# Attention feeding a squared-ReLU network: first-batch loads and projections in smaller parts, and one normalize moved a step earlier

## The chip, the cores and the metric

The kernel runs on one core of one Trainium2 chip. The metric is the device time of one execution in microseconds (us), so lower is better. Times are medians of several executions. A profiled execution also has a span, from its first to its last instruction; here the span is about 1.8 us shorter than the time of the same execution (482.0 against 483.81 in the profile of the kernel before).

Engines are named as the profile names them: PE is TensorE's matmul, PEld its weight load, DVE is VectorE, ACT is ScalarE, POOL is GpSimd (it issues most loads here), SP is SyncE.

## The reference

Linear attention with 64 projected keys feeds a two-layer network (cut to what matters):

```python
k_proj = np.einsum('ks,bhsd->bhkd', E, k)          # 8 batches, 8 heads, 1024 rows, head size 64
v_proj = np.einsum('ks,bhsd->bhkd', F, v)
scores = scale * np.matmul(q, k_proj.transpose(0, 1, 3, 2))
# ... softmax over the 64 projected keys
attn_out = np.matmul(attn, v_proj)
x = attn_out.transpose(0, 2, 1, 3).reshape(8192, 512)
h = np.maximum(x @ w_in, 0.0)                      # w_in is 512 x 2048
return h * h @ w_out                               # w_out is 2048 x 512
```

## The kernel before

Every batch is worked in "steps" of TensorE work of the two-layer network. The attention of the next batch is slipped in between those steps by tables that name a step and what to do there. Batches 2 to 6 carry the attention of the batch after them by the table `PIECES`. The first batch has nothing to hide behind: its attention stands ahead of the network, and so it is done in halves, and the first four blocks of the hidden layer are "opened" column group by column group as soon as parts of x exist.

The loads of the first batch, in the order in which they are issued:

```python
    def load_heads(t, src, g):
        s = slice(4 * g, 4 * g + 4)
        nc.gpsimd.dma_start(t[:, s], rows(src, 0)[:, s])
    # ...
    for g in range(2):
        load_heads(K_first, k, g)
    # ...
    load_q_half(0, slice(0, H))
    for g in range(2):
        load_heads(V_first, v, g)
    # ...
    for j in (0, 2, 1, 3):
        if j in (1, 3):
            load_q_half(1, slice(0, 4) if j == 1 else slice(4, 8))
        for g in range(2):
            nc.gpsimd.dma_start(w_in_sb[j][:, g], w_in_view[:, g, :, j * fw:(j + 1) * fw])
```

The stages of the first batch. `filler` is spare TensorE work, there only to keep the engine busy:

```python
        def first_stages(self):
            # ... filler
            self.project_k(0)
            # ... transpose_k(0), project_k(1), transpose_k(1), filler between
            for g in range(2):
                self.half_transpose_q(0, g, ffn_psum)
            for g in range(2):
                self.half_scores(0, g)
                self.half_exponentials(g)
            self.project_v(0)
            self.copy_v(0)
            self.half_sums(0, apart=True)
            self.half_sums(1)
            self.half_reciprocals(0)
            self.half_reciprocals(1)
            self.half_values(0)
            self.half_normalize(0, 0, 0)
            self.project_v(1)
            self.copy_v(1)
            self.half_normalize(0, 0, 1)

        def last_of_first(self):          # called one step into the network
            self.half_values(1)
            self.half_normalize(0, 1, 0)
            self.half_normalize(0, 1, 1)
```

The opening of the first four hidden blocks; `cb` is one of four column groups of x, and each normalize makes one of them:

```python
                def rest():
                    opening((3,), (0,))
                    for cb in range(1, NCB):
                        opening(range(4), (cb,), cb == NCB - 1)
                steps[0:4] = [lambda: opening(range(3), (0,)), rest, lambda: None, lambda: None]
```

The table for batches 2 to 6, and the two pools in PSUM (the memory that matmuls write to, in banks) whose buffers decide who waits:

```python
    aps = ctx.enter_context(tc.tile_pool(name="aps", bufs=2, space=bass.MemoryType.PSUM))   # attention
    fps = ctx.enter_context(tc.tile_pool(name="fps", bufs=4, space=bass.MemoryType.PSUM))   # network
    # ...
    PIECES = {
        # ...
        23: "sums 0, values 0 0, reciprocals 0", 26: "normalize 0 0",
        28: "scores 2, scores 3, exponentials 2", 29: "exponentials 3",
        # ...
    }
```

The softmax here doesn't subtract the row's maximum and nothing guards it: scores larger than these inputs give would overflow.

Of the kernel before, what the change touches and what calls it, by code (L numbers as in the profile page):

```python
# [8 lines left out]
P = 128  # L9
F32 = mybir.dt.float32  # L10
BF16 = mybir.dt.bfloat16
AF = mybir.ActivationFunctionType
# [8 lines left out]
def kernel(  # L21
# [11 lines left out]
    nc = tc.nc  # L33

    B, H, S, D = q.shape
    KP = E.shape[0]
    C = H * D
# [5 lines left out]
    NCB = C // P  # L43
# [29 lines left out]
    def ffn_psum(name, shape=(P, 512), dtype=F32):  # L73
        return fps.tile(list(shape), dtype, tag="ffn", name=name)

    def rows(src, b):
        return src[b].rearrange("h (p i) d -> p h (i d)", i=NI)
# [7 lines left out]
    for src in (E, F):  # L85
        t = relu_pool.tile([KP, S], F32, tag="h_relu", name="e_f32")
        nc.sync.dma_start(t[:], src[:])
        e_f32.append(t)
    K_first, V_first, Q_first = (
        qkv_pool.tile([P, H, NI * D], BF16, name=n) for n in ("K_sb", "V_sb", "Q_sb"))  # L90

    def load_heads(t, src, g):
        s = slice(4 * g, 4 * g + 4)
        nc.gpsimd.dma_start(t[:, s], rows(src, 0)[:, s])

    def load_q_half(c, h):
        s = slice(c * TH, (c + 1) * TH)
        nc.gpsimd.dma_start(Q_first[:, h, s], rows(q, 0)[:, h, s])

    for g in range(2):  # L100
        load_heads(K_first, k, g)
    ident = const_pool.tile([P, P], BF16, name="ident")
    make_identity(nc, ident[:])
    load_q_half(0, slice(0, H))
    for g in range(2):
        load_heads(V_first, v, g)
    nc.scalar.preload_act_table_set("natural_log_exp_and_others")
    ones = const_pool.tile([P, 32], BF16, name="ones")
    nc.vector.memset(ones[:], 1.0)
# [3 lines left out]
    w_in_view = moe_w_in.rearrange("(g p e) f -> p g e f", p=P, e=2)  # L113
    w_out_view = moe_w_out.rearrange("(fb p) m -> p fb m", p=P)
    WP = 4
    fw = FF // WP
    w_in_sb = [wpool.tile([P, 2, 2, fw], BF16, name=f"w_in_{j}") for j in range(WP)]
    wo = [wpool.tile([P, HFB, DM], BF16, name=f"w_out_{j}") for j in range(2)]
    for j in (0, 2, 1, 3):
        if j in (1, 3):  # L120
            load_q_half(1, slice(0, 4) if j == 1 else slice(4, 8))
        for g in range(2):
            nc.gpsimd.dma_start(w_in_sb[j][:, g], w_in_view[:, g, :, j * fw:(j + 1) * fw])
    for n in range(4):
        nc.gpsimd.dma_start(
            wo[n // 2][:, 4 * (n % 2):4 * (n % 2) + 4, :], w_out_view[:, 4 * n:4 * n + 4, :])
# [1 line left out]
    def w_in_blk(cb, fb):  # L128
        n = fw // P
        return w_in_sb[fb // n][:, cb // 2, cb % 2, (fb % n) * P:(fb % n + 1) * P]  # L130

    ET, FT = (const_pool.tile([P, NI, KP], BF16, name=n) for n in ("ET", "FT"))

    def E_and_F():
# [17 lines left out]
        o, a, b = {"T1": (T1, W12, W11), "T2": (T2, W22, T1), "T3": (T3, W22, W12), "T4": (T4, W21, T2)}[name]  # L152
        nc.vector.tensor_tensor(out=o[:, js], in0=a[:, js], in1=b[:, js], op=ALU.subtract)

    LO, HI = slice(0, 64), slice(64, 128)

    PLACE = {(0, 0): (LO, 0), (0, 1): (HI, 0), (1, 0): (HI, 1), (1, 1): (LO, 1)}

    class Attention:
# [111 lines left out]
                )  # L271
            nc.vector.tensor_copy(self.kT[:, s], ps[:])

        def project_v(self, g):
            if g == 0:
                self.vp = proj_pool.tile([P, H, 2, D // 2], BF16, name="vp")
            s = slice(4 * g, 4 * g + 4)
            ps = self.ps["vp", g] = ffn_psum("ps_v", (P, C // 2))
            vv = self.V[:, s].rearrange("p h (i d) -> p h i d", i=NI)
            for i in range(NI):  # L280
                for o in (LO, HI):
                    nc.tensor.matmul(
                        ps[o, :], lhsT=FT[:, i, :], rhs=vv[:, :, i, :], start=i == 0, stop=i == NI - 1)

        def copy_v(self, g):
            s = slice(4 * g, 4 * g + 4)
            nc.vector.tensor_copy(
                self.vp[:, s].rearrange("k h e d -> k e h d"),
                self.ps["vp", g][:].rearrange("k (h d e) -> k e h d", h=H // 2, e=2))

        def half_transpose_q(self, c, g, psum):
            ps = psum("ps_q", (P, 4, 2, P), BF16)
# [63 lines left out]
        def first_stages(self):  # L356
            def filler(n):
                ps = ffn_psum("ps_fill")
                for _ in range(n):
                    nc.tensor.matmul(ps[:], lhsT=ET[:, 0:2, :], rhs=ET[:], start=True, stop=True)  # L360

            filler(2)
            self.project_k(0)
            filler(1)
            self.transpose_k(0)
            self.project_k(1)
            filler(2)
            self.transpose_k(1)
            filler(1)
            for g in range(2):  # L370
                self.half_transpose_q(0, g, ffn_psum)
            for g in range(2):
                self.half_scores(0, g)
                self.half_exponentials(g)
            self.project_v(0)
            self.copy_v(0)
            self.half_sums(0, apart=True)
            self.half_sums(1)
            self.half_reciprocals(0)
            self.half_reciprocals(1)  # L380
            self.half_values(0)
            self.half_normalize(0, 0, 0)
            self.project_v(1)
            self.copy_v(1)
            self.half_normalize(0, 0, 1)

        def last_of_first(self):
            self.half_values(1)
            self.half_normalize(0, 1, 0)
            self.half_normalize(0, 1, 1)  # L390

        def second_half(self, stage, g):
            if stage == 0:
# [15 lines left out]
    PIECES = {  # L409
        1: "copy_kp", 2: "copy_vp", 4: "copy_v_down",  # L410
        20: "scores 0, scores 1, exponentials 0", 21: "exponentials 1",
        23: "sums 0, values 0 0, reciprocals 0", 26: "normalize 0 0",
        28: "scores 2, scores 3, exponentials 2", 29: "exponentials 3",
        47: "values 0 1, sums 1, reciprocals 1", 48: "normalize 0 1",
        53: "values 1 0, values 1 1", 54: "normalize 1 0", 55: "normalize 1 1",
# [16 lines left out]
        53: "values 1 0, values 1 1", 54: "normalize 1 0", 55: "normalize 1 1",  # L432
    }
    SECOND_HALF = {
        1: "last_of_first", 7: "second_half 0 0", 9: "second_half 1 0", 10: "second_half 0 1",
        11: "second_half 2 0", 12: "second_half 1 1", 13: "second_half 3 0",
        15: "second_half 2 1", 16: "second_half 3 1",
    }
# [17 lines left out]
    def ffn_groups(b, xT):  # L456
        def first(ch, fb, ps, cbs):
            for cb in cbs:
                nc.tensor.matmul(  # L459
                    ps[:], lhsT=w_in_blk(cb, fb), rhs=xT[:, cb, :, 2 * ch:2 * ch + 2],  # L460
                    start=(cb == 0), stop=(cb == NCB - 1),
                )
# [24 lines left out]
        def chunk(ch):  # L487
# [9 lines left out]
            def begin():  # L497
                st["hsq"] = hsq_pool.tile([P, 2, HFB, TCH], BF16, name="hsq")
                if b:
                    begin_sums()  # L500
# [4 lines left out]
            def square(k, n, ps):  # L505
                hsq = st["hsq"]
                if n == 0:
                    st["r"] = relu_pool.tile([P, 2, TCH], F32, name="h_relu")
                r = st["r"]
                nc.scalar.activation(r[:, n], ps[:], AF.Relu)  # L510
                if n == 0:
                    return
                (h, j), (h1, _) = pairs[k]
                o = hsq[:, :, j, :] if h != h1 else hsq[:, h, j:j + 2, :]
                if k in ON_SCALAR.get((b, ch), ()):
                    nc.scalar.activation(o, r[:], AF.Square)
                    return operands_after(k)
                multiply = lambda: nc.vector.tensor_tensor(out=o, in0=r[:], in1=r[:], op=ALU.mult)  # L518
                if b == 0 and ch == 0 and k in (4, HFB - 1):
                    held.append(multiply)  # L520
                    return
                multiply()
                operands_after(k)

            def operands_after(k):
                if b and 4 <= k < 7:
                    operands(0, (k - 4,))
                if b and k == 7:
                    operands(0, (3,))
                    operands(1, (0,))  # L530
# [14 lines left out]
            def opening(fbs, cbs, last=False):  # L545

                if "open" not in st:
                    begin()
                    st["open"] = {}
                for n in fbs:  # L550
                    if n not in st["open"]:
                        st["open"][n] = ffn_psum("ps_h")
                    h, j = pairs[n // 2][n % 2]
                    first(ch, HFB * h + j, st["open"][n], cbs)
                    if last:
                        square(n // 2, n % 2, st["open"][n])

            steps = [lambda k=k, n=n: step1(k, n) for k in range(HFB) for n in range(2)]
            if b == 0 and ch == 0:
                def rest():  # L560
                    opening((3,), (0,))
                    for cb in range(1, NCB):
                        opening(range(4), (cb,), cb == NCB - 1)
                steps[0:4] = [lambda: opening(range(3), (0,)), rest, lambda: None, lambda: None]
            elif b + ch == 1:
                def two():
                    if held:
                        held.pop()()
                    opening((0, 1), (2,))
                    opening((0, 1), (3,), True)  # L570
                steps[0:4] = [lambda: opening(range(4), (0, 1)), two] + [
                    lambda n=n: opening((n,), (2, 3), True) for n in (2, 3)]
# [108 lines left out]
        steps = f0 + f1 + s0 + s1  # L681
# [69 lines left out]
```

## Time and profile before

| | before |
|---|---|
| time, median of 3 runs | 484.76 us (484.01 to 484.77) |
| span of the profiled execution | 482.0 us |
| TensorE busy with matmuls | 470.4 us, 98% |
| first opening matmul / last of the 16 | 20.01 / 23.70 us |
| a batch, from one to the next (batches 2 to 6) | 57.38 us |

From the page of the kernel before, the engines' busy time and the chain of waits by engine:

```profile
PE 470.4 (98%) x3614; PEld 293.1 (61%) x3614; DVE 313.2 (65%) x380; ACT 261.8 (54%) x414; POOL 33.2 (7%) x46
...
PE 93%; DVE 3%; ACT 2%; DMA 1%; issue 0%; SPq 0%
```

TensorE is the limit. But "98% busy" does not say how much is left to win: the Trainium skill, "Perfetto Trace Analysis", section "Identifying the Most-Contended Engine", says that matmul busy time is not a good measure of how close a kernel is to its limit, because matmuls are pipelined. This trace agrees: a 512-column matmul shows 0.38 us of duration, but the next one starts 0.216 us later. So only the distances between starts are read here. The 0.216 is also what "TensorE: Matmul & The Clock Gate", section "Wait — 56ns, not 53.3ns?", gives for 512 columns at the full clock (215.7 ns).

Now the timeline of the kernel before in the opening. The columns are start, length, engine, line, operation, output and inputs, count, and in brackets the engine's idle time before it and what ended it:

```profile
18.58 1.06 PE L282 MATMUL ps_v<-V_sb,FT 128*64 128x256 bf16 x16
...
19.27 0.69 DVE L350 TENSOR_TENSOR xT<-ps_att,rs 128x512 bf16<-128x512 f32 x1 [1.17 <-ACT rs L341]
...
19.88 0.41 DVE L287 CAST vp<-ps_v 128x256 bf16<-128x256 f32 x1
...
20.01 0.81 PE L459 MATMUL ps_h<-xT,w_in 128*128 128x512 bf16 x3 [0.37 <-DVE xT L350]
...
20.75 0.41 PE L319 MATMUL ps_att<-expT,vp 64*32 64x256 bf16 x16
...
21.10 4.26 PE L459 MATMUL ps_h<-xT,w_in 128*128 128x512 bf16 x18
...
22.01 1.79 PEld L459 LDWEIGHTS <-w_in 128*128 128x128 bf16 x9 [0.15 <-DMA w_in<-in_moe_w_in_dram]
```

TensorE projects the second half of V at 18.58, waits for the first normalize (19.27), starts three opening matmuls at 20.01, does the second group of values at 20.75 once V's copy (19.88) is done, and resumes the opening at 21.10. Some 0.5 us of idle time lie ahead of 20.01.

And the timeline of the kernel before at the second group of scores in batch 2, which is the same in batches 3 to 6:

```profile
164.41 0.69 DVE L595 TENSOR_TENSOR o_sb<-ps_z,p_b 128x512 f32<-128x512 f32 x1 [4.22 <-ACT p_b L591]
165.02 1.22 DVE L244 TENSOR_TENSOR xT<-ps_att,rs 128x1024 bf16<-128x1024 f32 x1
165.99 0.70 PE L204 MATMUL ps_att<-qT,kT 64*64 64x512 bf16 x8
...
166.29 0.11 PEld L204 LDWEIGHTS <-kT 64*64 64x64 bf16 x4 [0.18 <-DVE xT L244]
```

The normalize (line 244) stands behind an add (line 595) that can't start before 164.41. So it ends at 166.24. Its PSUM bank is what the second of the two score groups waits for: the groups start at 165.99 and 166.29, which is 0.30 apart, where the pair at 157.68 us, which waits for nothing, has 0.24.

### The profile page before, as it was taken

The page shows a single profiled execution, that of the slowest core. Times are in us where ns is not written, and L with a number is a line of the kernel's source. Part 1 is how long each engine was busy: PE and PEld are TensorE (multiplying, and loading weights), DVE is VectorE, ACT ScalarE, POOL GpSimd, SP SyncE. Part 2 cuts the span into 40 slices and gives each one's busy share as a digit, 9 for nine tenths or more (in the row PEclk, how much of TensorE's full clock was granted, in tenths as well). Part 3 has the DMA queues.
Part 4 walks back from the last instruction along what each step waited for, and adds up shares of the span by engine and source line. Part 5 has one row for each costly group of instructions (what it writes and reads, how often), then busy time and mean ns, then how long its engine had stood idle before and what let it go on. Part 6 is the DMA issues. An engine that isn't in the chain of part 4 may idle for free.

```text
span 482.0 us, 8383 instructions
## 1 busy us (share of the span) xinstructions
PE 470.4 (98%) x3614; PEld 293.1 (61%) x3614; DVE 313.2 (65%) x380; ACT 261.8 (54%) x414; POOL 33.2 (7%) x46
## 2 busy tenths in 40 slices
PE   4899999999999999999999999999999999999997
PEld 2544776475575746657475665747557474666656
DVE  1478855555958558493876748666594855948383
ACT  2488544758426664466635657176662756545351
POOL 6340020020020001000010000100000000000000
PEclk9999999999999999999999999999999999999999
DMA  9999989479989075931859147590712002020202
GB/s 162 204 204 207 170 184 203 124 128 227 172 124 238 6 176 89 192 80 64 145 87 229 13 121 131 90 196 1 173 3 81 20 1 88 1 88 0 88 0 88
DMA packets 72501, 55.46 MB, mean 115 GB/s; under 512 B 33936, under 2 KB 64656, under 8 KB 72464
## 3 DMA queue, kind: packets, MB, share of 16 engines
q0 software_dynamic: 30336, 29.36, 39.0%
q1 hardware_dynamic: 42128, 25.56, 21.2%
q8 instruction: 28, 0.46, 0.4%
q14 instruction: 9, 0.07, 0.0%
HBM read 59.24 MB, written 16.78 MB: 158 GB/s over the span
## 4 chain that ended last, share of the span: by engine, by line
PE 93%; DVE 3%; ACT 2%; DMA 1%; issue 0%; SPq 0%
PE ps_h L459 44%; PE ps_y L479 23%; PE ps_z L479 11%; PE ps_x L479 6%; PE ps_kv L178 3%; PE ps_att L219 2%; PE ps_att L204 2%; DVE hsq L518 1%; DMA e_f<-in_F_dram 1%; PE ps_k L260 1%; DVE s L473 1%; DVE xT L244 0%; ACT expT L313 0%; DVE xT L350 0%; ACT h_relu L510 0%; PE ps_fill L360 0%
## 5 line engine op out<-in xcount | busy, mean ns | idle before, releaser
L459 PE MATMUL ps_h<-xT,w_in 128*128 128x512 bf16 x1024 | 225.0, 379 | 0.4 <-DVE xT L350 0.4
L518 DVE TENSOR_TENSOR hsq<-h_relu 128x1024 bf16<-128x1024 f32 x123 | 150.0, 1223 | 76.7 <-ACT h_relu L510 76.1
L510 ACT ACTIVATE h_relu<-ps_h 128x512 f32<-128x512 f32 x256 | 149.8, 597 | 62.6 <-PE ps_h L459 62.4
L459 PEld LDWEIGHTS <-w_in 128*128 128x128 bf16 x1024 | 99.6, 98 | 117.9 <-issue 1.7
L479 PEld LDWEIGHTS <-s 128*128 128x128 bf16 x1024 | 98.5, 98 | 19.8 <-issue 8.7
L479 PEld LDWEIGHTS <-hsq 128*128 128x128 bf16 x768 | 73.8, 98 | 16.4 <-issue 2.9
L479 PE MATMUL ps_y<-T,s 128*128 128x256 bf16 x512 | 62.4, 273 | 0.0
L595 DVE TENSOR_TENSOR o_sb<-ps_z,p_b 128x512 f32<-128x512 f32 x16 | 11.1, 691 | 54.7 <-ACT p_b L591 21.1
L473 DVE TENSOR_TENSOR s<-hsq 128x1024 bf16<-128x1024 bf16 x64 | 43.5, 684 | 0.0
L591 ACT COPY o_sb<-ps_y 128x512 f32<-128x512 f32 x15 | 8.8, 586 | 54.2 <-PE ps_y L479 54.1
L211 ACT ACTIVATE expT<-ps_att 128x1024 bf16<-128x1024 f32 x28 | 27.2, 1025 | 14.0 <-PE ps_att L204 14.0
L244 DVE TENSOR_TENSOR xT<-ps_att,rs 128x1024 bf16<-128x1024 f32 x28 | 33.4, 1216 | 0.6 <-PE ps_att L219 0.6
L479 PE MATMUL ps_x<-w_out,hsq 128*128 128x256 bf16 x256 | 33.2, 273 | 0.0
L479 PE MATMUL ps_y<-w_out,hsq 128*128 128x256 bf16 x256 | 33.2, 273 | 0.0
L479 PE MATMUL ps_y<-T,hsq 128*128 128x256 bf16 x256 | 30.9, 272 | 0.0
L479 PE MATMUL ps_z<-T,s 128*128 128x256 bf16 x256 | 30.6, 273 | 0.0
L479 PE MATMUL ps_z<-w_out,s 128*128 128x256 bf16 x256 | 30.6, 273 | 0.0
L591 ACT COPY p_b<-ps_y 128x512 f32<-128x512 f32 (+1 forms) x17 | 9.4, 556 | 25.9 <-PE ps_y L479 25.8
L473 DVE TENSOR_TENSOR s<-s,hsq 128x1024 bf16<-128x1024 bf16 x32 | 21.9, 686 | 0.3
L473 DVE TENSOR_TENSOR s<-hsq,s 128x1024 bf16<-128x1024 bf16 x32 | 21.8, 684 | 0.0
L81 POOL DMA_DIRECT2D Q_sb<-in_q_dram x7 | 6.1, 877 | 226.1 <-DMA qT<-Q_sb 225.7
L591 ACT COPY p_a<-ps_y 128x512 f32<-128x512 f32 (+1 forms) x17 | 9.4, 561 | 21.8 <-PE ps_y L479 21.6
(74 smaller groups left out, 232.0 us busy)
## 6 DMA issues: line engine op xcount, KB each, us to landing
out_dram<-o_sb SPq DMA_DIRECT2D x30, 512.0 KB, 3.1
K_sb<-in_k_dram POOLq DMA_DIRECT2D x7, 1024.0 KB, 15.4
V_sb<-in_v_dram POOLq DMA_DIRECT2D x7, 1024.0 KB, 22.4
Q_sb<-in_q_dram POOLq DMA_DIRECT2D x7, 1024.0 KB, 9.8
w_in<-in_moe_w_in_dram POOLq DMA_DIRECT2D x8, 256.0 KB, 13.6
w_out<-in_moe_w_out_dram POOLq DMA_DIRECT2D x4, 512.0 KB, 13.3
K_sb<-in_k_dram POOLq DMA_DIRECT2D x2, 512.0 KB, 7.9
V_sb<-in_v_dram POOLq DMA_DIRECT2D x2, 512.0 KB, 12.7
```

The source lines that it names most:

```text
L178: nc.tensor.matmul(ps[0:KP, :], lhsT=ET[:, i, :], rhs=kv[:, :, i, :], start=f, stop=l)
L204: nc.tensor.matmul(ps[o, bank, :], lhsT=self.kT[r, 2 * pr + j, :], start=True, stop=True, rhs=self.qT[r, NT * (2 * pr + j):NT * (2 * pr + ...
L211: nc.scalar.activation(e[:], self.ps["s", pr][:], AF.Exp, scale=SCALE)
L219: nc.tensor.matmul(ps[32 * j:32 * j + 32, a, :], lhsT=weights(o, 4 * g + j), rhs=self.exp[2 * g + j // 2][o, bank, :], start=True, stop=Tr ...
L244: nc.vector.tensor_tensor(out=self.xT[:, 2 * g + e].rearrange("p a n t -> p a (n t)"), in0=self.ps["v", g, e][:], in1=self.rs[g][:], op=AL ...
L459: nc.tensor.matmul(ps[:], lhsT=w_in_blk(cb, fb), rhs=xT[:, cb, :, 2 * ch:2 * ch + 2], start=(cb == 0), stop=(cb == NCB - 1),)
L473: nc.vector.tensor_tensor(out=s[o][:, js], in0=x, in1=y, op=op)
L479: nc.tensor.matmul(ps[tb] if len(ps) == 2 else ps[0][:, tb], lhsT=lhs[:, j, tb * P:(tb + 1) * P], rhs=rhs[:, j], start=first and n == 0 an ...
L510: nc.scalar.activation(r[:, n], ps[:], AF.Relu)
L518: multiply = lambda: nc.vector.tensor_tensor(out=o, in0=r[:], in1=r[:], op=ALU.mult)
L591: nc.scalar.copy(to[:, t], ps)
L595: nc.vector.tensor_tensor(out=to[:, t], in0=ps, in1=more[:, t], op=ALU.add)
```

## The change

The intent has two parts. In the opening, the second half of V is loaded, projected and copied in two parts of two heads each; the first load of w_in is halved as well; and both groups of values go ahead of the opening, which then runs without a break. One ReLU of the opening moves from ScalarE to VectorE. In batches 2 to 6, `normalize 0 0` goes from step 26 to step 25, ahead of the add in VectorE's order.

```diff
-    for g in range(2):
-        load_heads(V_first, v, g)
+    for s in (slice(0, 4), slice(4, 6), slice(6, 8)):
+        load_heads(V_first, v, s)
 ...
         for g in range(2):
-            nc.gpsimd.dma_start(w_in_sb[j][:, g], w_in_view[:, g, :, j * fw:(j + 1) * fw])
+            for n in range(2) if (j, g) == (0, 0) else (slice(None),):
+                s = slice(n * fw // 2, (n + 1) * fw // 2) if n in (0, 1) else n
+                nc.gpsimd.dma_start(
+                    w_in_sb[j][:, g, :, s], w_in_view[:, g, :, j * fw:(j + 1) * fw][:, :, s])
 ...                                              # project_v and copy_v take a slice of heads
-            self.project_v(0)
-            self.copy_v(0)
+            heads = [slice(0, 4), slice(4, 6), slice(6, 8)]
+            self.project_v(heads[0])
+            self.copy_v(heads[0])
 ...
             self.half_values(0)
-            self.half_normalize(0, 0, 0)
-            self.project_v(1)
-            self.copy_v(1)
-            self.half_normalize(0, 0, 1)
-
-        def last_of_first(self):
+            for s in heads[1:]:
+                self.project_v(s)
+                self.copy_v(s)
             self.half_values(1)
-            self.half_normalize(0, 1, 0)
-            self.half_normalize(0, 1, 1)
+            for g in range(2):
+                for e in range(2):
+                    self.half_normalize(0, g, e)
 ...
-        23: "sums 0, values 0 0, reciprocals 0", 26: "normalize 0 0",
+        23: "sums 0, values 0 0, reciprocals 0", 25: "normalize 0 0",
 ...
-        1: "last_of_first", 7: "second_half 0 0", ...
+        7: "second_half 0 0", ...
 ...
-                nc.scalar.activation(r[:, n], ps[:], AF.Relu)
+                if (b, ch, k, n) == (0, 0, 0, 1):
+                    nc.vector.tensor_scalar_max(r[:, n], ps[:], 0.0)
+                else:
+                    nc.scalar.activation(r[:, n], ps[:], AF.Relu)
 ...
-                def rest():
-                    opening((3,), (0,))
-                    for cb in range(1, NCB):
-                        opening(range(4), (cb,), cb == NCB - 1)
-                steps[0:4] = [lambda: opening(range(3), (0,)), rest, lambda: None, lambda: None]
+                steps[0:4] = [
+                    lambda cb=cb: opening(range(4), (cb,), cb == NCB - 1) for cb in range(NCB)]
```

## The prediction

> **What bounds it now.** TensorE. The engine table gives it 470.4 of 482.0 us (98%), and the chain of waits is 93% TensorE. Since busy matmul time overstates (the Trainium skill, "Perfetto Trace Analysis", § Identifying the Most-Contended Engine), I used the distance between matmul starts. In the feed-forward stages a 512-column matmul follows another every 0.216 us, which is what the skill's "TensorE: Matmul & The Clock Gate" gives for a warm clock (N / 2.4 GHz + 2.5 ns; trace and page agree). So only start-to-start excess can be won.
>
> Excess in reach of this change, from the timeline of before:
> - Opening, 18 to 24 us: 0.54 us before the first opening matmul (20.01), 0.09 around the second values group (20.75), 0.20 where block 8 waits for a ReLU to free its bank (24.11).
> - Batches 2 to 6, at the second of two score groups (166.29, 223.67, 281.06, 338.44, 395.82): 0.07 us, plus about 0.02 behind it. The normalize ends at 166.24, its bank is the one awaited. Five times 0.09 is 0.45 us.
>
> **Opening, after.** V's second group lands at 18.54 us; its projection takes 18.58 to 19.64, but its copy only starts at 19.88, behind a normalize (0.69). After: the first part (lands near 17.3, an estimate) is projected right behind the first values group, from about 18.45; 128-column pairs at 0.055 us (as the transposes show) give 0.45 per part, the second runs to about 19.3. Copies (256 columns took 0.42; 128 should take 0.28) end near 19.8. But now both copies stand ahead of the first normalize on VectorE, so it starts near 19.75 instead of 19.27, and a matmul follows 0.74 us after its start: opening at about 20.5, not 20.0. The 16 opening matmuls then run unbroken (16 x 0.216) and the last starts near 23.73; before it was 23.70. So the early start with three matmuls and the gap are traded for a later, dense block: about zero.
>
> It also cannot gain much: w_in's second piece lands at 21.97 and the third and fourth opening columns need it (before they reach it at 22.19); the next at 23.0 and 24.3, the latter used at 24.54. The load stream, not the order, sets this stage; splitting loads moves no bytes and 512-byte packets (as Q's) move as many GB/s here. A 16 KB instruction fetch at 19.72 delays one DMA engine by about 0.9 us; it will come slightly earlier, with margin.
>
> The ReLU on VectorE takes about 0.69 us instead of 0.60 on ScalarE but in parallel: the first square comes some 0.15 us earlier; TensorE waits for block 0's ReLU, not this one, so nothing is gained on the chain.
>
> **Steady stage.** The normalize one step earlier runs ahead of an add that waits until 164.4; its reciprocals are ready at 163.56. It ends near 164.8, before the scores at 166.0. The 5 x 0.09 us go. The add moves about 0.35 us later, uncritical.
>
> **Sum.** -0.45 (steady) and 0.0 +- 0.25 (opening) against a level of about 484.5: I predict **484.1 us, range 483.4 to 484.9**; faster by over 2% 0.01, within 2% 0.98, slower 0.01.
>
> **Right if:** scores pairs in batches 2 to 6 start 0.22 us apart instead of 0.285; the batch period falls from 57.38 to about 57.29; first opening matmul near 20.5, last near 23.7; block 8 still waits about 0.2 us for the ReLU. **Wrong if:** the opening starts near 20.0 (then up to 0.3 us more won), if the split loads land late so that opening columns wait, if the delayed add makes a new wait in the product steps, or if the first batch's later halves stall on VectorE.

## The result, and the profile after

| | before | after |
|---|---|---|
| time, median of 6 runs on the same chip | 484.61 us (484.01 to 485.0) | 484.10 us (483.60 to 484.55) |
| ratio, 95% interval | | 0.999 (0.9977 to 1.0003): the same |
| span of the profiled execution | 482.0 us | 482.4 us |
| first opening matmul / last of the 16 | 20.01 / 23.70 us | 21.05 / 24.29 us |
| a batch (batches 2 to 6) | 57.38 us | 57.30 us |

The time fell inside the predicted range. Note a trap, though: the profiled execution of the new kernel was 0.4 us longer than that of the old one. Whoever compares only the two profiles reads the wrong sign.

From the page of the kernel after:

```profile
PE 470.3 (97%) x3630; PEld 292.6 (61%) x3630; DVE 314.1 (65%) x382; ACT 261.5 (54%) x413; POOL 34.7 (7%) x48
...
PE 92%; DVE 3%; DMA 3%; ACT 1%; POOL 1%; issue 0%; POOLq 0%
```

The sum of TensorE's work is unchanged, with 16 more matmuls for the halved V. The chain of waits now has 3% of DMA.

The timeline of the kernel after in the opening:

```profile
18.75 1.32 PE L284 MATMUL ps_v<-V_sb,FT 128*64 128x128 bf16 x32
...
19.43 0.48 PEld L284 LDWEIGHTS <-FT 128*64 128x64 bf16 x16 [0.21 <-DMA V_sb<-in_v_dram]
...
20.11 0.29 DVE L288 CAST vp<-ps_v 128x128 bf16<-128x128 f32 x1 [0.39 <-PE ps_v L284]
20.32 2.47 DVE L351 TENSOR_TENSOR xT<-ps_att,rs 128x512 bf16<-128x512 f32 x4
...
20.46 0.41 PE L320 MATMUL ps_att<-expT,vp 64*32 64x256 bf16 x14 [0.16 <-DVE vp L288]
...
21.05 4.24 PE L459 MATMUL ps_h<-xT,w_in 128*128 128x512 bf16 x18 [0.19 <-DVE xT L351]
...
24.71 0.31 PEld L459 LDWEIGHTS <-w_in 128*128 128x128 bf16 x2 [0.32 <-issue]
```

The new order is there as intended: V in two parts with copies of 0.29 us, all four normalizes in one row, and an opening that starts later and runs unbroken. The last line, with the 0.20 us before it in the starts of matmuls (24.29 plus 0.216, but 24.70), is the block that follows the first four (block 8 by number) waiting for a bank that a ReLU must empty; that wait was there before too.

The opening came 0.59 us later than in the profile of before, by block 8's start (24.70 against 24.11). The loads explain that: V's first group landed at 16.78 instead of 16.00, and its last part at 19.39 instead of 18.54. The split does not explain the lateness of V: K's first load, which the change does not touch, was already late (8.72 instead of 8.25), and over all traces with full loads V's first group lands 7.74 to 8.06 us after K's first with the new loads (after, e2, e3, e5, e6, e11) and 7.74 to 7.90 with the old (before, e1, e7, e12). From V's first group to its last part it is 2.59 to 2.65 instead of 2.54 or 2.55.

Measured from the last landing of V, the opening's end was 0.26 us earlier (4.90 instead of 5.16). That compares one execution with one, and in before the opening did not wait for V's landing but for the normalize and the work ahead of it, so it does not show a gain.

The timeline of the kernel after at the second group of scores:

```profile
164.37 1.22 DVE L246 TENSOR_TENSOR xT<-ps_att,rs 128x1024 bf16<-128x1024 f32 x1 [3.41 <-ACT rs L236]
165.51 0.68 DVE L595 TENSOR_TENSOR o_sb<-ps_z,p_b 128x512 f32<-128x512 f32 x1
...
166.77 0.63 PE L206 MATMUL ps_att<-qT,kT 64*64 64x512 bf16 x8
```

The normalize is ahead of the add and ends at 165.59. The two score groups are now one row, 0.24 us apart, and the bracket that named the normalize is gone.

One more stage differed: at 53 us TensorE projects K and V of batch 2 side by side, each on half of the array. In the timeline of the kernel after, restricted to TensorE's matmuls (and below it the first two lines of the same stage in before):

```profile
53.03 0.40 PE L180 MATMUL ps_kv<-K_sb,ET 128*64 128x512 bf16 x1
53.32 0.38 PE L181 MATMUL ps_kv<-V_sb,FT 128*64 128x512 bf16 x1
53.32 0.40 PE L180 MATMUL ps_kv<-K_sb,ET 128*64 128x512 bf16 x1
```

```profile
52.44 0.40 PE L178 MATMUL ps_kv<-K_sb,ET 128*64 128x512 bf16 x1
52.53 0.38 PE L179 MATMUL ps_kv<-V_sb,FT 128*64 128x512 bf16 x1
```

V's half starts 0.29 us after K's, and the stage, up to the first product after it, took 2.11 us; in the profile of before V followed K by 0.09 us and the stage took 1.91. So the two profiles differ by +0.59 (opening) +0.20 (this stage) −0.41 (steady batches) = +0.38 us, which is, to rounding, the 482.38 against 482.01 of the spans. Only the last term is in every run, as the experiments show; the middle one comes back in every trace that has the new loads unaltered and no spare matmuls (see e12).

### The profile page after: what moved, and what is told of

It is laid out like the page before. It is cut to its first block, busy times and chain, and to the rows that moved or that the text cites. A ratio compares the mean times of both kernels' runs of the same rounds, so it can differ in the third digit from the quotient of the medians.

```text
span 482.4 us, 8423 instructions
## 1 busy us (share of the span) xinstructions
PE 470.3 (97%) x3630; PEld 292.6 (61%) x3630; DVE 314.1 (65%) x382; ACT 261.5 (54%) x413; POOL 34.7 (7%) x48
## 3 DMA queue, kind: packets, MB, share of 16 engines
HBM read 59.24 MB, written 16.78 MB: 158 GB/s over the span
## 4 chain that ended last, share of the span: by engine, by line
PE 92%; DVE 3%; DMA 3%; ACT 1%; POOL 1%; issue 0%; POOLq 0%
PE ps_h L459 44%; PE ps_y L479 23%; PE ps_z L479 11%; PE ps_x L479 6%; DMA V_sb<-in_v_dram 3%; PE ps_kv L180 2%; PE ps_att L221 2%; PE ps_att L206 2%; DVE hsq L521 1%; DVE s L473 1%; PE ps_v L284 0%; DVE xT L246 0%; DVE xT L351 0%; PE ps_kv L181 0%; ACT h_relu L513 0%; POOL K_sb L93 0%
## 5 line engine op out<-in xcount | busy, mean ns | idle before, releaser
L246 DVE TENSOR_TENSOR xT<-ps_att,rs 128x1024 bf16<-128x1024 f32 x28 | 33.4, 1215 | 17.6 <-ACT rs L236 17.0
```

The costliest lines, as they stand in the source:

```text
L246: nc.vector.tensor_tensor(out=self.xT[:, 2 * g + e].rearrange("p a n t -> p a (n t)"), in0=self.ps["v", g, e][:], in1=self.rs[g][:], op=AL ...
```

## The experiments

**The theories.** The one on record says: the steady batches win 5 × 0.09 us; the opening is worth about zero, because an earlier start is traded for an unbroken block, and because the load stream sets that stage. The rivals: (a) the opening loses or wins through its order on the engines, independent of the loads; (b) the profiled executions differ by something that neither part of the change touches, such as the time at which the clock is granted; (c) the gain of the moved normalize is not in the normalize.

The table holds the marks of all profiled executions that the verdicts use, all read from the traces, in us. "Clock" is the trace's first record of a fully granted TensorE clock; before that date the matmuls start at half the rate (0.213 us apart for 256 columns instead of 0.109, see e6), which is called the slow clock below. "V starts" is the first matmul of V's projection. "Work" is the time from there to the last of the 16 opening matmuls. "Rest" is the span after the first product of the second layer (it starts near 55 us), so it contains the steady batches and nothing of the opening.

| run | clock | V group 1 landed | V starts | last opening | work | rest | span |
|---|---|---|---|---|---|---|---|
| before | 12.37 | 16.00 | 16.57 | 23.70 | 7.13 | 427.66 | 482.01 |
| after | 11.23 | 16.78 | 16.82 | 24.29 | 7.47 | 427.24 | 482.38 |
| e1_norm_only | 17.61 | 17.01 | 18.84 | 25.95 | 7.11 | 427.25 | 483.79 |
| e2_opening_only | 12.09 | 15.84 | 16.32 | 23.59 | 7.27 | 427.65 | 482.15 |
| e3_norm_late | 12.43 | 16.55 | 16.70 | 24.48 | 7.78 | 433.85 | 489.24 |
| e4_half_k | 13.80 | 14.52 | 17.61 | 24.87 | 7.26 | 427.25 | 482.71 |
| e5_pairwise | 12.25 | 15.88 | 16.49 | 23.75 | 7.26 | 427.22 | 481.88 |
| e6_warm | 6.42 | 15.62 | 15.66 | 23.73 | 8.07 | 427.25 | 481.57 |
| e7_old_order_warm | 9.50 | 15.80 | 15.96 | 23.46 | 7.50 | 427.25 | 481.54 |
| e8_v_whole | 15.37 | 15.96 | 17.68 | 25.05 | 7.37 | 427.25 | 482.90 |
| e9_warm_half_k | 4.25 | 13.00 | 14.65 | 21.91 | 7.26 | 427.24 | 479.74 |
| e10_all | 4.96 | 15.74 | 15.78 | 24.10 | 8.32 | 427.26 | 481.75 |
| e11_after_again | 13.84 | 17.38 | 18.09 | 25.35 | 7.26 | 427.23 | 483.45 |
| e12_norm_again | 12.42 | 15.75 | 16.60 | 23.73 | 7.13 | 427.27 | 481.60 |

### e1_norm_only: the moved normalize alone

```diff
 # against before
-        23: "sums 0, values 0 0, reciprocals 0", 26: "normalize 0 0",
+        23: "sums 0, values 0 0, reciprocals 0", 25: "normalize 0 0",
```

> Before with the one table entry moved (normalize of batches 2 to 6 at step 25), nothing of the opening. Theory A (the gain is the five steady waits): 0.39 us faster than before (5 x 0.078, the batch period falls from 57.38 to 57.30 us), pairs of score groups 0.22 us apart in batches 2 to 6. Rival B (the gain is the opening): same as before within 0.1 us, though the pairs may close.

Measured: 485.07 us (483.86 to 485.55, 5 runs) beside 484.65 of before (11 runs), ratio 1.0006 (0.999 to 1.0022). The time missed. The profile shows why the time can't be used: the steady part did shrink, 427.25 instead of 427.66, but in this execution the clock was granted at 17.61 us instead of 12.37, and the opening ended 2.25 us later. Not all of that is the clock: K's first load landed later too (9.27 instead of 8.25), and K's projection started 0.70 us later. Of the 2.27 us by which V's projection started later, the other 1.57 arose between the two. The timeline of e1 has all of K, and then Q's transposes, at the slow clock:

```profile
12.26 1.91 PE L260 MATMUL ps_k<-K_sb,ET 128*64 128x256 bf16 x8
...
15.80 1.91 PE L295 MATMUL ps_q<-ident,Q_sb 128*128 128x128 bf16 x16
```

The timeline of before has the same two groups at 11.61 and 14.23:

```profile
11.61 1.42 PE L260 MATMUL ps_k<-K_sb,ET 128*64 128x256 bf16 x8
...
14.23 1.06 PE L295 MATMUL ps_q<-ident,Q_sb 128*128 128x128 bf16 x16
```

Rival (b) was born here: the date of the clock grant differs between executions by up to 6 us, and with it the time moves by more than this change is worth.

### e2_opening_only: all but the normalize

```diff
 # against after
-        23: "sums 0, values 0 0, reciprocals 0", 25: "normalize 0 0",
+        23: "sums 0, values 0 0, reciprocals 0", 26: "normalize 0 0",
```

> After with the normalize back at step 26: loads, projections, order of the opening and the ReLU as in after. Theory A: within 0.2 us of before on average, the waits of 0.07 us back in batches 2 to 6, period 57.38 us; measured from the landing of V's first group the last opening matmul starts 7.5 to 7.7 us later (before 7.70, after 7.51). Rival B: about 0.5 us faster than before.

Measured: 484.45 us (483.91 to 485.99, 6 runs), ratio 1.0001 (0.9985 to 1.0017). The rest is 427.65, as in before: the new opening does nothing to the steady batches. The last opening matmul came at 23.59 against 23.70; a wait of 0.10 us for w_in and the stage at 53 us (2.03 us instead of 1.91) took that back. The new opening is worth about nothing in time, as the prediction had it.

### e3_norm_late: the normalize two steps later than before

```diff
 # against after
-        23: "sums 0, values 0 0, reciprocals 0", 25: "normalize 0 0",
-        28: "scores 2, scores 3, exponentials 2", 29: "exponentials 3",
+        23: "sums 0, values 0 0, reciprocals 0",
+        28: "normalize 0 0, scores 2, scores 3, exponentials 2", 29: "exponentials 3",
```

> After with that normalize at step 28, behind the second add of the products, so that its bank comes free late. If the place of the normalize on VectorE sets the wait of the second score group (theory A): that group starts about 1.8 us later in each of batches 2 to 6 (add until 166.8, normalize 1.2 us), 9 us slower in all, range 7 to 10. If the 0.07 us gap was a cost of TensorE's own (rival: spacing of groups, not a wait): no change.

Measured: 490.91 us (490.27 to 492.23, 4 runs), ratio 1.0133 (1.0114 to 1.0151); the rest is 433.85. That is 6.6 us in five batches, less than expected. The timeline of e3 shows that the bank that is waited for changed:

```profile
167.03 0.41 PE L206 MATMUL ps_att<-qT,kT 64*64 64x512 bf16 x4
...
167.74 1.22 DVE L246 TENSOR_TENSOR xT<-ps_att,rs 128x1024 bf16<-128x1024 f32 x1
168.56 0.41 PE L206 MATMUL ps_att<-qT,kT 64*64 64x512 bf16 x4 [1.13 <-ACT expT L213]
```

The second score group now waits for the exponential of the first (released at 168.51), not for the normalize, which ends later, at 168.96. The pool has two buffers, and the normalize still reads one of them when the second group starts, so that group must have taken the first group's bank: the later place of the normalize turned the order of the buffers around. The groups start 1.54 us apart instead of 0.24; 5 × 1.30 = 6.5 us. So the normalize's place does set the distance of the score groups, which speaks against rival (c), but my expected size (9 us, 7 to 10) took the wrong wait.

### e4_half_k: half of K's load taken away

The second half of K's heads is never loaded and the first half is used twice. Its output is wrong, which doesn't matter for the time. (The comparison accepted it all the same. With inputs scaled by 0.1 the softmax is nearly flat, an estimate from the reference's scales, so K hardly shows in the output.) All later loads come earlier by half a megabyte.

```diff
 # against after
-    for s in (slice(0, 4), slice(4, 8)):
+    for s in (slice(0, 4),):
         load_heads(K_first, k, s)
 ...
-            kv = self.K[:, s].rearrange("p h (i d) -> p h i d", i=NI)
+            kv = self.K[:, 0:4].rearrange("p h (i d) -> p h i d", i=NI)
```

> Wrong result on purpose: after without the load of K's second head group (heads 4 to 7 of batch 0 use the first group's K), so that 512 KB of written bytes leave the front of the load stream, 2.6 us by the landings of before. If the load stream alone sets the opening (as I predicted): all later landings and the opening come 2 to 2.6 us earlier, and the time falls by 2 to 2.6 us. If the chain of TensorE, VectorE and ScalarE work is nearly as long as the stream (rival): the landings come 2.6 us earlier, but the opening only 0.1 to 0.7 us, and so the time.

Measured: 484.12 us (483.11 to 484.48, 5 runs), ratio 0.9983 (0.9966 to 0.9999) against before, not to be told apart from the new kernel (484.10, ratio 0.999). V landed at 14.52, over 2 us earlier than in after, but its projection started at 17.61 only. From e4's chain of waits, limited to the first 27 us (start, length, what):

```profile
1.25 8.05 DMA K_sb<-in_k_dram
...
9.34 1.88 PE ps_k L262 x8
...
12.36 1.73 PE ps_k L262 x8
...
17.13 1.95 ACT expT L314 x2
```

From 9.30 on there is no load in the chain, only work: K's projections, at the slow clock, the copies, Q, the exponentials. This refutes a part of the prediction: "The load stream, not the order, sets this stage" does not hold as a statement about one limit. Taking a piece out of the load stream alone bought nothing. (One caveat: the first load of K, which the edit does not touch, landed at 9.30 in this execution, later than the 8.25 of before and the 8.72 of after. That is less than the 3 us by which V was early, and e9 below repeats the test.)

For comparison, the same view of the kernel before: its summary line, and three pieces of the chain.

```profile
by line: PE ps_h L459 24.0%; DMA e_f<-in_F_dram 16.7%; PE ps_k L260 11.9%; ACT expT L313 7.2%; PE ps_fill L360 4.8%; ACT e_bf L137 3.9%; DVE kp L262 3.2%; DVE qT L298 2.6%; DVE xT L350 2.6%; PE ps_E L141 2.6%; PE ps_kT L269 2.5%; ACT rs L34
...
1.38 4.51 DMA e_f<-in_F_dram
...
8.68 1.86 PE ps_k L260 x8
...
16.09 1.94 ACT expT L313 x2
```

And of the kernel after:

```profile
4.21 12.57 DMA V_sb<-in_v_dram
...
16.82 1.06 PE ps_v L284 x16
```

In the profiled execution of before the chain is work from 5.9 us on; in that of after it is V's load up to 16.78. V's load ended 0.57 us before its projection in the one, 0.04 in the other. Two limits, the work and the loads, are nearly equally long, and which one wins is decided by the execution.

### e5_pairwise: the opening finished in pairs

The last two column groups are done block by block, so that block 0's ReLU can empty its bank earlier.

```diff
 # against after
-                steps[0:4] = [
-                    lambda cb=cb: opening(range(4), (cb,), cb == NCB - 1) for cb in range(NCB)]
+                steps[0:4] = [
+                    lambda: opening(range(4), (0,)), lambda: opening(range(4), (1,)),
+                    lambda: (opening((0, 1), (2,)), opening((0, 1), (3,), True)),
+                    lambda: [opening((n,), (2, 3), True) for n in (2, 3)]]
```

> After, with the opening's last columns in another order: blocks 0 and 1 take both of them before blocks 2 and 3 do, so that block 0 is finished 0.43 us sooner. If block 8 waits for block 0's ReLU and for nothing else (theory A): the 0.20 us excess ahead of the 17th feed-forward matmul goes in the trace, 0.2 us faster, unless the next w_in piece has not landed. Rival (it waits for w_in or for the ReLU of block 1): the excess stays.

Measured: 483.75 us (483.34 to 484.14, 5 runs) beside 484.51 (11 runs), ratio 0.9982 (0.9969 to 0.9995). The wait of 0.20 us for the ReLU is gone (23.75 to 23.97 is one matmul), but the next wait is right behind it, in the timeline of e5:

```profile
24.69 1.19 PEld L459 LDWEIGHTS <-w_in 128*128 128x128 bf16 x7 [0.63 <-DMA w_in<-in_moe_w_in_dram]
```

A w_in piece landed at 24.65 and TensorE lost 0.30 us to it. In the trace the loads took back more than the repaired wait; the span still came out at 481.88. In e10 below, which has the same finish and where that piece landed at 24.12, neither wait is left.

### e6_warm: the clock granted early

Eleven spare matmuls on a constant tile, eight ahead of E's transposes and three behind, so that the clock is granted before K arrives.

```diff
 # against after
+    warm = const_pool.tile([P, 512], BF16, name="warm")
+    nc.vector.memset(warm[:], 1.0)
+    def warm_up(n):
+        ps = ffn_psum("ps_warm")
+        for _ in range(n):
+            nc.tensor.matmul(ps[:], lhsT=warm[:, 0:P], rhs=warm[:], start=True, stop=True)
 ...
     def E_and_F():
+        warm_up(8)
 ...
             copy(t[:], ps[:])
+            if t is ET:
+                warm_up(3)
```

> After, with 11 spare 512-column matmuls on a constant tile, 8 ahead of the first transposes and 3 behind them, while TensorE has nothing else to do. Theory C (the profiled runs so far got the full TensorE clock at 11.2 to 17.6 us, and that time, with the landing of the first K group, makes most of the scatter between runs and the late start of the single-part runs): full clock by about 9 us, K's matmuls 0.107 us apart instead of 0.213, V's projection within 0.1 us of the landing of V's first group, a median 0.3 to 1.0 us below after, and a smaller spread of the five runs. Rival (the landings alone make the scatter): the clock may come earlier, but time and spread stay.

Measured: 483.75 us (483.57 to 485.27, 6 runs), ratio 0.9987 (0.9973 to 1.0001). The median is 0.35 us below that of after; the smaller spread that was expected missed (1.7 us, where after has 0.95). They were run at other times. From the timeline of e6, K's first projection and the opening:

```profile
7.94 1.06 PE L272 MATMUL ps_k<-K_sb,ET 128*64 128x256 bf16 x8
...
20.91 5.98 PE L469 MATMUL ps_h<-xT,w_in 128*128 128x512 bf16 x26 [0.42 <-DMA w_in<-in_moe_w_in_dram]
```

The same group of eight took 1.92 us in before, from its timeline:

```profile
8.61 1.92 PE L260 MATMUL ps_k<-K_sb,ET 128*64 128x256 bf16 x8
```

The matmuls start 0.109 us apart in e6 and 0.213 apart in before. That is nearly the factor of two that "TensorE: Matmul & The Clock Gate", section "What's actually happening", states for the cold and the warm clock. (The row of the granted clock on the profile's page reads 9 in every slice of all runs: a slice is 12 us long, and the row does not show this.) Now V's projection starts with V's landing (15.66 against 15.62): the work is no longer the limit, the loads are. And then a piece of w_in came late: it landed at 20.86 and cost 0.58 us of matmul starts (the first two matmuls start at 19.90 and 20.12, so the third was due at 20.33; the 0.42 in the bracket counts from the modelled end of the second).

Why did it come late? In the other traces with that split the two halves of the first load of w_in landed 0.63 to 0.68 us apart; in e6 it took 1.96. In the view of DMA queues of e6 between 17 and 24 us there is one instruction fetch:

```profile
q8 instruction: 1, 0.02, 0.8%
```

That is one packet of 16 KB, and 0.8% of 16 engines over 7 us is 0.9 us on one engine. "DMA: Bandwidth & Descriptors", section "Queues, rings and completion order", says that each engine alternates between its queues packet by packet, so a load's share on that engine would stand behind the fetch. "Runtime: NRT & Kernel Launch", section "Instruction fetch mechanics", calls the cost of crossing such a block of instructions "mostly hidden"; here, if the fetch is the cause, it is not hidden from a load that is just in time. That the fetch delays the piece is read from the dates of both; no run here moved the fetch by itself. The other traces support it in part. Each has one such fetch in this stretch, which starts between 18.1 and 22.1 us. In ten of the fourteen (before, e2, e3, e5 to e10, e12) exactly one landing of w_in is 0.7 to 1.3 us late behind its predecessor, and it comes 2.1 to 2.6 us after the start of the fetch. In the other four (after, e1, e4, e11) the fetch is there and no piece is late. In e3, where the opening is that of after, such a piece (22.91) cost TensorE 0.41 us.

### e7_old_order_warm: the old opening with early clock, moved normalize and pairwise finish

```diff
 # against before: warm_up as in e6, "normalize 0 0" at step 25 as in e1, and
-                    for cb in range(1, NCB):
-                        opening(range(4), (cb,), cb == NCB - 1)
+                    opening(range(4), (1,))
+                    opening((0, 1), (2,))
+                    opening((0, 1), (3,), True)
+                    for n in (2, 3):
+                        opening((n,), (2, 3), True)
```

> Before's opening (V whole, three matmuls ahead of the second values group, ReLU on ScalarE) with the normalize at step 25, the pairwise finish and the spare matmuls. If the new order of the opening costs 0.1 us rather than winning (from the runs so far 7.26 us from V's projection to the last opening matmul, 7.12 in before's order): as fast as or up to 0.3 us faster than the same without the old order, about 1 us faster than before. If the new opening is worth something: slower than e6 in spite of the pairwise finish.

Measured: 483.68 us (483.31 to 484.20, 5 runs), ratio 0.9983 (0.9969 to 0.9998). The old order, without any split load, reaches the same time as the new order with one of the helps (e5, e6) or with both (e10). Once the loads are the limit, the order of the opening is not worth anything that these runs can resolve.

### e8_v_whole: the new order, V's second half in one piece

```diff
 # against after
-    for s in (slice(0, 4), slice(4, 6), slice(6, 8)):
+    for s in (slice(0, 4), slice(4, 8)):
         load_heads(V_first, v, s)
 ...
-            heads = [slice(0, 4), slice(4, 6), slice(6, 8)]
+            heads = [slice(0, 4), slice(4, 8)]
```

> After with V's second group in one load, one projection and one copy, the new order kept. One look, read from the trace alone: the copy then takes 0.42 us instead of the last 0.29 and the projection ends no earlier, so from V's first projection to the last opening matmul 7.35 to 7.45 us (after's order without a load wait 7.26, before 7.12). If the split of V wins nothing: 7.26 or less.

One look: 484.67 us, state unknown, not used as a time. In its trace, where no load was waited for behind the start of V's projection, the work took 7.37 us. The three steps compare: 7.13, 7.11 and 7.13 in the old order (before, e1, e12); 7.37 in the new order with V whole; 7.26 or 7.27 in the new order with V split (e2, e4, e5, e9, e11). So, by this one execution, the new order alone (with the split of w_in and the moved ReLU) costs 0.24 us of work, the split of V gives 0.11 back, and 0.13 to 0.14 us remain as loss in all these traces, where no load is waited for. That supports rival (a) in mechanism, inside the ±0.25 of the prediction in size.

### e9_warm_half_k: both limits lifted

The edits of e4 and of e6 together. Its output is wrong, which doesn't matter for the time.

```diff
 # against after: warm_up as in e6, and half of K as in e4
```

> Wrong result on purpose: the spare matmuls and the shortened K load together, on after. If two limits of nearly the same length stand behind the opening, the chain of work (longer when the TensorE clock comes late) and the load stream, then lifting both moves what lifting one did not: V's projection near 15.4 us, last opening matmul near 22.7 us (23.6 to 24.3 with one limit lifted or none, 24.9 with a late clock), no wait for w_in, 0.8 to 1.3 us faster than the kernel with the spare matmuls alone. If something else holds the opening: no better than 483.7 us.

Measured: 481.81 us (481.66 to 483.6, 6 runs) beside 484.56 (11 runs), ratio 0.995 (0.9934 to 0.9966). This is the clearest run: less load alone (e4) gave 484.12, the clock alone (e6) 483.75, both together 481.81. Two limits of nearly the same length stand side by side, and lifting either leaves the other. The gain over e6 is 1.94 us, more than the 0.8 to 1.3 expected. From the timeline of e9:

```profile
14.65 1.06 PE L294 MATMUL ps_v<-V_sb,FT 128*64 128x256 bf16 x16
...
18.68 1.02 PE L469 MATMUL ps_h<-xT,w_in 128*128 128x512 bf16 x4 [0.19 <-DVE xT L361]
```

V's projection starts 1.0 us earlier than in e6 and the opening 1.2 us earlier; w_in is not waited for.

### e10_all: e5 and e6 together, w_in's first load whole

```diff
 # against after: warm_up as in e6, the opening as in e5, and
-            for n in range(2) if (j, g) == (0, 0) else (slice(None),):
+            for n in (slice(None),):
```

> The best correct version that the runs point to: after with the pairwise finish, the spare matmuls and w_in's first piece in one load again (its second part came 0.8 us late behind an instruction fetch in the run with the spare matmuls, and TensorE waited 0.58 us). Expected 483.5 us, 483.2 to 483.9, since the j=2 w_in pieces land near 24.2 us and block 8 then waits for them: as good as the old order with the same additions (483.68), not clearly better.

Measured: 483.70 us (483.59 to 484.69, 6 runs), ratio 0.9987 (0.9972 to 1.0001). The part of the expectation that TensorE would not wait for w_in missed: the whole first load landed at 20.81, behind a fetch as in e6. The first opening matmul came at 20.85; with the 0.73 us that e6 has from the start of the first normalize to the first opening matmul, it was due at 20.02, so TensorE waited 0.83 us for w_in where e6 with the halves waited 0.58. The opening's work is 8.32 instead of 8.07 us, the same difference. So splitting w_in's first load is worth 0.25 us in such an execution (one trace of each kernel), and nothing where the load is early enough (e2, e5).

### e11_after_again and e12_norm_again: repeats for the scatter

No edit against the kernel after, and none against e1.

> The changed kernel once more, unchanged, on the same chip as the two above, for its time beside them and a second trace. 484.1 us, 483.6 to 485.5 by the time of the clock grant. If the grant comes early (under 12.5 us) and the loads are not late, the last opening matmul 7.26 us after V's first projection as in the other kernels of this order; if the loads are late, the distance to the landing of V's last part is 4.9 us.

> The first experiment's kernel once more (before with the normalize at step 25), since its five runs were 0.4 us slower than before, against the 0.39 us that its trace shows won after the opening (427.25 us from the first ps_x product to the end, before 427.66). If those runs only met late clock grants: now 484.1 to 484.4 us, faster than before by 0.2 to 0.6 us, and the same 427.25 in the trace. If something in that program makes its opening late every time: again near 485.0 us with a grant after 15 us.

Measured: e11 483.99 us (483.86 to 485.22, 6 runs), ratio 0.9994 (0.998 to 1.0008). e12 484.36 us (483.40 to 485.20, 6 runs), beside 484.34 of before (11 runs), ratio 0.9993 (0.9961 to 1.0025). So the time of e12 again shows no gain of the moved normalize, where 0.2 to 0.6 us were expected; only the trace does. In the trace of e11 both limits came late: K's first load landed at 9.64 and the clock was granted at 13.84.

The trace of e12 is the pair to before that e1 was not: clock granted at 12.42 and 12.37, V's projection at 16.60 and 16.57, opening finished at 23.73 and 23.70. What remains is nearly the moved normalize alone: the spans are 481.60 and 482.01, 0.41 us, of which 0.39 lie in the rest. From the timeline of e12 in batch 2:

```profile
163.57 1.23 DVE L244 TENSOR_TENSOR xT<-ps_att,rs 128x1024 bf16<-128x1024 f32 x1 [3.40 <-ACT rs L234]
...
165.97 0.63 PE L204 MATMUL ps_att<-qT,kT 64*64 64x512 bf16 x8
```

The score groups form one row, as in the kernel after. And at the stage of K and V near 53 us, the timeline of e12 restricted to TensorE's matmuls shows what it is like when both loads are there:

```profile
52.48 0.40 PE L178 MATMUL ps_kv<-K_sb,ET 128*64 128x512 bf16 x1
52.48 0.40 PE L179 MATMUL ps_kv<-V_sb,FT 128*64 128x512 bf16 x1
```

Both halves start together, and the stage takes 1.85 us instead of the 2.11 of the kernel after. There V's load landed at 53.27, after TensorE wanted it at 53.03. Whether that belongs to the change is open. The stage took 1.99 to 2.13 us in all five traces that have the new loads unaltered and no spare matmuls (after, e2, e3, e5, e11), and 1.85 to 1.91 in the three that have the old loads and none (before, e1, e12). But it took 2.12 in e7, with the old loads and the clock early, and 1.85 in e6, with the new loads and the clock early, and also in e4, e8, e9 and e10, where other loads were altered. From K's first landing to that of V for batch 2 it is 44.0 to 44.5 us with the old loads (before, e1, e7, e12) and 44.4 to 44.9 with the new (after, e2, e3, e5, e6, e11). So the split loads may cost up to 0.3 us here; no run tested it.

**What stays open.** The parts can't be told apart by their times. All 50 runs of before have a median of 484.50, the 12 of after (with e11) 484.01, the 11 of e1 and e12 484.94, spread over 483.4 to 485.55; these are no strict comparison. They were run at other times. The traces carry the argument, not these medians. Why some executions get their loads 0.5 to 1 us later, and why even with the early clock one of the six runs of e6, of e9 and of e10 is 1.0 to 1.8 us above the median of its kernel, was not found. The fastest correct versions (e5, e6, e7, e10) stand at 483.68 to 483.75 and can't be told apart.

## Why the prediction was right, point by point

- **The total** was right: 484.1 predicted, 484.10 measured. With a scatter of half a microsecond from run to run, the exact hit is luck; the range is what counts.
- **The steady batches** were right in mechanism and nearly in size. Predicted 5 × 0.09 = 0.45 us; measured about 0.4 us, by the rest after the first product (427.66 and 427.65 with the old place, 427.22 to 427.27 in all kernels with the normalize at step 25) and by the pair before and e12 (0.39 in the rest). The predicted spacing, counted as the prediction does from the last start of the first group, was 0.22 us and is 0.23, and the period of 57.29 is 57.30. The overstated term is the wait of 0.07: the spacing fell by 0.055 only (0.285 to 0.23), while the "about 0.02 behind it" is there (0.024, from the second group to the product after it, before against e12). That makes 0.08 per batch where 0.09 was summed.
- **The opening's worth of 0.0 ± 0.25** was right. It costs 0.14 us where the work is the limit (7.27 against 7.13). Whether it wins where the loads are the limit is not shown: from V's last landing after took 4.90 us, and e7, in the old order, 5.11, but e7 also waited about 0.3 us for w_in ahead of its first opening matmul. The reason given, an early start traded for an unbroken block, is what the traces show.
- **"The load stream, not the order, sets this stage"** was half right. e4 took load away and won nothing, e6 gave the clock early and won little, e9 did both and won 2.75 us against before. There are two limits of nearly the same length. The prediction did not look at the one that belongs to TensorE: K projected at the slow clock.
- **The dates of 20.5 and 23.7 us** for the opening's start and end missed in the profiled execution (21.05 and 24.29), because its loads came 0.8 us later at V. In e2 and e5, whose loads came earlier, they were 20.35 and 23.59, and 20.52 and 23.75: right.
- **The wait of block 8 for a ReLU** stayed at 0.20 us, as predicted; e5 shows that removing it can hand the wait to a w_in piece, e10 that it need not.
- **The instruction fetch "with margin"** was wrong, as far as the dates tell. In before the late piece cost nothing, but in e3, e6 and e10 the w_in piece that came late behind the fetch was the one that TensorE needed next, at 0.41, 0.58 and 0.83 us of waiting. The prediction named late split loads, so that "opening columns wait", as a sign of being wrong: that did not happen in the profiled execution of after, but in e6 the late piece was a split one.
- **Not foreseen at all:** the clock's date, between 11.2 and 17.6 us in kernels without spare matmuls, and V's late load at 53 us. The first moves an execution by more than the whole change does, the second by up to 0.28 us.

## What to carry to other kernels

When a change is worth less than the run-to-run scatter, look for a stretch of the trace that contains only that change (here the span after the first product) and for a pair of executions whose start-up marks agree; the whole times and a single pair of profiles can show the wrong sign. When a start-up phase doesn't react to lifting its named limit, lift the second candidate together with the first before giving the theory up: here the medians of each alone are 0.5 and 0.8 us below before, of which the change itself makes 0.5, and both together gave 2.75 us. Moving a buffer's last reader ahead of an instruction that waits is free gain if the buffer is what the critical engine asks for next, but check which buffer that will be after the move.

## What the Trainium skill lacked or had wrong

- "TensorE: Matmul & The Clock Gate", section "What's actually happening": the two speeds agree (0.213 and 0.109 us for 256 columns), and so does its warning that the warm-up varies and costs below 1% of the span (e1, with the latest grant, lost 1.57 us against before between K's and V's projections, 0.3%). But it names ±500 ns for the date of the grant. In nine traces without spare matmuls that have K's full load (before, after, e1, e2, e3, e5, e8, e11, e12), with TensorE working from 5.0 to 5.6 us on in broken stretches, the grant came between 11.2 and 17.6 us. The page gives its figure for sustained activity, so this is a case that it leaves out rather than an error. What it says of broken activity is about a clock that is lost again between loop iterations; a start-up that stays cold for up to 6 us longer in one execution than in another is not there.
- "Runtime: NRT & Kernel Launch", section "Instruction fetch mechanics": it calls the cost of crossing a block of instructions "mostly hidden". It does not say what the fetch does to loads: 16 KB took about 0.9 us on one DMA engine, and in ten of fourteen traces a load landed 0.7 to 1.3 us late 2.1 to 2.6 us after the fetch began (1.96 instead of 0.63 to 0.68 us behind its predecessor in e6), for which TensorE waited 0.58 us in e6 and 0.83 us in e10. That the fetch is the cause is not shown.
- "TensorEngine Tiling (Array Packing)", section "Key Properties": that tiles work independently agrees (K and V start together at 52.48 us in e12). No page gives the price of one operand landing late in such a pair: V starting 0.29 us behind K made the stage 2.11 instead of 1.85 us long.
- No page has a way to tell two start-up limits of nearly the same length apart; here it took a run that lifted both (e9, 481.81 us, where e4 and e6 with one lifted have 484.12 and 483.75).
